# Two weight-tail loads laid out with an outermost extent of 8 in a one-core decode kernel

## The chip, the cores and the metric

The kernel runs on one core of a Trainium2 chip. A time is the device time of one execution in microseconds. Before and after were each run 6 times beside each other; the experiments were timed 4 times each, beside 7 runs of the kernel before on the same chip. A ratio is the mean time of one kernel's fast runs over that of the other's of the same rounds, so it is not quite the ratio of the medians quoted. A span in the profile leaves out some 2 us at the ends (before: 382.6 us span, 384.72 us median).

Besides the views of the profile I use the trace's records of single DMA packets (start, duration, bytes, queue). A packet here is one row: 32768 B for keys and values, 36864 B for the main rows of gate, up and wo, 4608 B for the last 64 rows of gate and up ("the tails"), 10368, 6912 and 3456 B for W_down. A 4 B packet is the completion write of one DMA engine for one load. The records do not name the engine. I chained them by their times (a row starts within a few ns of the end of the one before on the same engine) and by the order of the queue; chains can swap engines that stand within some ns of each other. Packet sums by engine below, and which engines carried what, rest on that; packet durations do not.

## The reference, cut to what matters

```python
def reference(A_x, A_k_cache, A_v_cache, A_wq, A_wo, B_x, B_W_gate, B_W_up, B_W_down):
    x = A_x                                        # 4 rows of 576
    h = x + attention(layernorm(x), ...)           # 32 heads, 16 KV heads, window of 4096 of 16384
    # second block, all weights bf16
    n = layernorm(h)
    gate = n @ B_W_gate                            # 576 x 4608
    up = n @ B_W_up                                # 576 x 4608
    return h + (where(gate > 0, gate, 0) * up) @ B_W_down    # 4608 x 576
```

128 MiB of keys and values and about 25 MB of weights are read once, for 4 rows of input.

## The kernel before: the parts that matter

All large loads go to one queue in program order: keys and values in 32 loads of 4 MiB (wq after the first), with wo before the last value load, then gate, up and W_down. A weight of 576 rows is split: its first 512 rows lie four to a partition, its last 64 are cut in halves and fill all 128 partitions.

```python
def main_rows(W):
    return W[0:512, :].rearrange("(p r) n -> p (r n)", r=4)

def last_rows(W):
    return W[512:576, :].rearrange("r (a n) -> (r a) n", a=2)     # partition 2r + a
...
# add_kv: outermost extent of the source 32, four partitions to each
src = cache[b, 4 * qd:4 * qd + 4, SK - WIN:SK, :].rearrange("a (p t) d -> p a (t d)", p=32)
...
for g, W in ((0, B_W_gate), (1, B_W_up)):
    for m, n, src in ((1, F // 2, last_rows(W)), (0, 4 * F, main_rows(W))):
        gu_off[(g, m)] = off
        place(("gu", g, m), off, n, ("GU", g, m),
              lambda e, off=off, n=n, src=src: e.dma_start(out=arena[:, off:off + n], in_=src))
        off += n
...
# the tail's input chunk is masked, once for each half a of the row
for a in range(2):
    dve("n3", lambda e, a=a: e.tensor_scalar(out=hnT[:, 4 + a, 0:4], in0=tmp5[:, 4, :],
                                             scalar1=par[:, a:a + 1], scalar2=None, op0=ALU.mult), ...)
```

Of the kernel before, what the change touches and what calls it, by code (L numbers as in the profile page):

```python
# [6 lines left out]
ALU = mybir.AluOpType  # L7
AX = mybir.AxisListType
FP32 = mybir.dt.float32
BF16 = mybir.dt.bfloat16  # L10

B = 4
D = 576
# [5 lines left out]
F = 4608  # L19
# [95 lines left out]
def bass_sequential_preLN__sliding_block_cached__glu_gated_reglu__decode_kernel(  # L115
# [12 lines left out]
    with ExitStack() as es:  # L128
        cnt = [0]

        def sb(name, shape, dt):
            return es.enter_context(nc.sbuf_tensor("sb_" + name, shape, dt))
# [3 lines left out]
        dve = lambda name, fn, deps=(): P.op("vector", name, fn, deps)  # L136
# [12 lines left out]
        c_qm = sb("c_qm", [128, 4, 32], FP32)  # L149
# [2 lines left out]
        perm = sb("perm", [128, 4, 32], BF16)  # L152
        m4 = sb("m4", [128, 4], FP32)
        par = sb("par", [128, 2], FP32)
        am8 = sb("am8", [128, 8], FP32)
        qm = sb("qm", [128, 4], FP32)
        e8 = sb("e8", [128, 8], FP32)
# [5 lines left out]
        warm = sb("warm", [128, 2], FP32)  # L163
        x_bf = sb("x_bf", [B, D], BF16)
        xn_bf = sb("xn_bf", [B, D], BF16)
        xd_bf = sb("xd_bf", [B, 64, 2], BF16)
        xnd_bf = sb("xnd_bf", [B, 64, 2], BF16)
        bn = sb("bn", [B, 2, 6], FP32)
        mv = sb("mv", [B, 8], FP32)
# [11 lines left out]
        hnT = sb("hnT", [128, DC + 1, 32], BF16)  # L181
        R_sb = sb("R_sb", [128, DC, 2, B], FP32)
        st2 = sb("st2", [128, 40], FP32)
        tmp5 = sb("tmp5", [128, DC, B], FP32)
# [6 lines left out]
        partd = pp[:, 1152:1408].bitcast(FP32)  # L191
# [7 lines left out]
        psb = es.enter_context(nc.psum_tensor("psb", [128, 8, 512], FP32))  # L199
# [39 lines left out]
                  lambda e: e.dma_start(out=arena[:, off:off + TILE], in_=src), key=f"slot{s}")  # L239


        def main_rows(W):
            return W[0:512, :].rearrange("(p r) n -> p (r n)", r=4)

        def last_rows(W):
            return W[512:576, :].rearrange("r (a n) -> (r a) n", a=2)

        P.dma("scalar", ("L", "x"), lambda e: e.dma_start(out=x_bf[:, :], in_=A_x.rearrange("b s d -> (b s) d")), "d_x")
        add_kv("K", 0)
# [17 lines left out]
        gu_off = {}  # L267
        off = WO_OFF + H * D
        for g, W in ((0, B_W_gate), (1, B_W_up)):
            for m, n, src in ((1, F // 2, last_rows(W)), (0, 4 * F, main_rows(W))):  # L270
                gu_off[(g, m)] = off
                place(("gu", g, m), off, n, ("GU", g, m), lambda e, off=off, n=n, src=src: e.dma_start(out=arena[:, off:off + n], in_=src))
                off += n
        WDJ = 9 * D
        wd_off = []
        for j in range(4):
            wd_off.append(off)
            for r0, r1 in ((0, 9),) if j < 3 else ((0, 6), (6, 9)):
                place(("wd", j, r0), off + r0 * D, (r1 - r0) * D, "DOWN",
                      lambda e, off=off, j=j, r0=r0, r1=r1: e.dma_start(  # L280
                          out=arena[:, off + r0 * D:off + r1 * D],
                          in_=B_W_down[j * 1152:(j + 1) * 1152, :].rearrange("(p r) n -> p (r n)", p=128)[:, r0 * D:r1 * D]))
            off += WDJ

        def kv(kind, i):
# [24 lines left out]
                                                in_=c_qm[:, :, :].rearrange("p q (h j) -> p q h j", j=4),  # L310
# [20 lines left out]
        for q in range(4):  # L331
# [9 lines left out]
                                               op0=ALU.mult, op1=ALU.add), ["c_par0"])  # L341
        dve("c_am8", lambda e: e.tensor_copy(out=am8[:, :].rearrange("p (a h) -> p a h", h=2),
                                             in_=bass.AP(tensor=m4, offset=0, ap=[[4, 128], [1, 4], [0, 2]])), ["c_m4"])
# [4 lines left out]
        for hf in range(2):  # L348
# [6 lines left out]
                                            op0=ALU.subtract, op1=ALU.mult), ["rstd"])  # L355
        act("warm_exp", lambda e: e.activation(out=warm[:, 1:2], in_=eps_c[:, :], func=ACT.Exp), ["std"])

        dve("xd", lambda e: e.tensor_copy(out=xd_bf[:, :, :], in_=bass.AP(tensor=x_bf, offset=512, ap=[[D, B], [1, 64], [0, 2]])))
        dve("xnd", lambda e: e.tensor_copy(out=xnd_bf[:, :, :], in_=bass.AP(tensor=xn_bf, offset=512, ap=[[D, B], [1, 64], [0, 2]])),
            ["xn"])  # L360

# [1 line left out]
        def chunk(t, td, c):  # L363
            return td if c == 4 else t[:, 0:512].rearrange("b (p r) -> b r p", r=4)[:, c, :]
# [3 lines left out]
        def pe_q():  # L368
            for c in range(DC):
                pe("TP0", lambda e, c=c: e.transpose(out=tpv[:, c * 4:(c + 1) * 4],  # L370
                                                     in_=chunk(xn_bf, xnd_bf[:, :, :].rearrange("b r a -> b (r a)"), c),
                                                     identity=ident_b[0:B, 0:B]), ["xnd", "xd", "c_idb"] if c == 0 else [])
            for c in range(DC):
                pe("TP1", lambda e, c=c: e.transpose(out=tpv[:, 32 + c * 4:32 + (c + 1) * 4],
                                                     in_=chunk(x_bf, xd_bf[:, :, :].rearrange("b r a -> b (r a)"), c),
                                                     identity=ident_b[0:B, 0:B]))
            for c in range(DC):
                for n in range(8):
                    g, bk = n % 4, n // 4
                    w = arena[:, wq_off + c * H * DH + n * 512:][:, 0:512] if c < 4 else pT[:, n % 4 * 512:n % 4 * 512 + 512]  # L380
                    pe("QMM", lambda e, c=c, w=w, g=g, bk=bk: e.matmul(
                        bank[4 + bk][32 * g:32 * g + 32, :], lhsT=xnT[:, c + bk if c == 4 else c, :], rhs=w,
                        start=(c == 0), stop=(c == DC - 1), skip_group_check=True),
                        ([("L", "wq", c // 4)] + (["xnT", "c_xnT"] if c == 0 else [])) if n == 0 and c % 4 == 0 else [])
            for bk in range(2):
                for s in range(4):
                    blk = bk * 4 + s
                    pe(("QT", blk), lambda e, blk=blk: e.transpose(out=mb_ps[:, blk * 128:(blk + 1) * 128],
                                                                   in_=p_sb[:, blk * 128:(blk + 1) * 128], identity=ident_b[:, :]),
                       [f"qev{bk}"] if s == 0 else [])  # L390
# [17 lines left out]
        def act_q():  # L408
            act("qev1", lambda e: e.copy(out=p_sb[:, 512:1024], in_=bank[5]), ["QMM"])
# [152 lines left out]
        for s in range(NUNIT + 16):  # L562
            b, k = divmod(s - 16, 16)
            if b >= 0 and k == 3:
                put_pT(b, 2)
            if s < NUNIT:
                pe_tr(s)
                for j in range(4):
                    evac(s, j)
            if b >= 0 and k == 1:  # L570
                softmax(b, 1)
            if s == 3:
                pe_q()
                act_q()
                dve_q()
                dve("c_qm", lambda e: e.tensor_reduce(out=qm[:, :], in_=c_qm[:, :, :], axis=AX.X, op=ALU.max), ["c_qm1"])
                dve("c_e8", lambda e: e.tensor_reduce(out=e8[:, :], in_=c_e8[:, :, :], axis=AX.X, op=ALU.max), ["c_e81"])
                dve("c_sel", lambda e: e.tensor_reduce(out=sel4[:, 0:4], in_=c_s4[:, :, :], axis=AX.X, op=ALU.max),
                    ["c_s41", "c_sel0"])
                for q in range(4):  # L580
                    dve("c_selc", lambda e, q=q: e.tensor_copy(out=selc[:, q, :, q], in_=e8[:, :]), ["c_e8", "c_selc0"])
                pe_qk(0)
            elif s >= 4 and s % 2 == 0 and s // 2 - 1 < NUNIT // 2:
                dd = s // 2 - 1
                pe_qk(dd)
                if dd % 8 == 7:
                    softmax(dd // 8, 0)
            if b >= 0:
                if k == 0 and b:
                    finish_o(b - 1)  # L590
                elif 1 <= k <= 3:
                    put_pT(b, (0, 1, 3)[k - 1])
                elif 4 <= k < 8:
                    weights(b, k - 4)
                if k % 4 == 3:
                    for w in range(4):
                        pe_pv(s - 19 + w)
                    select_o((s - 19) // 4)
# [5 lines left out]
        for a in range(8):  # L604
            for j in range(4):
                for n in range(2):
# [3 lines left out]
                        [("ONORM", B - 1), ("L", "wo"), ("EV", NUNIT - 1, 0), ("EV", NUNIT - 1, 1)] if a == j == n == 0 else [])  # L610
        dve("part0", lambda e: e.tensor_copy(out=part[:, 0:288], in_=bank[0][:, 0:288]), ["WO", ("PV", NUNIT - 1)])
        act("part1", lambda e: e.copy(out=part[:, 288:576], in_=bank[1][:, 0:288]), ["WO", ("PV", NUNIT - 1)])  # L612
        dve("partd", lambda e: e.tensor_copy(out=partd.rearrange("p (r a) -> p r a", a=2),
                                             in_=bass.AP(tensor=psb, offset=512 + 224, ap=[[4096, 128], [1, 64], [0, 2]])), ["part1"])
        for c in range(DC):
            pe("HT", lambda e, c=c: e.matmul(m_ps[:, c * 4:(c + 1) * 4], lhsT=chunk(part, partd, c), rhs=sel4[:, 0:4],
                                             start=True, stop=True), ["part0", "part1", "partd", "c_sel"] if c == 0 else [])
# [1 line left out]
                                            in1=xT[:, :, :], op=ALU.add), ["HT", "xT"])  # L619
# [16 lines left out]
        dve("n2a", lambda e: e.tensor_tensor(out=tmp5[:, :, :], in0=tmp5[:, :, :], in1=rstd_bc, op=ALU.mult), ["n1", "s6"])  # L636
        dve("n2", lambda e: e.tensor_copy(out=hnT[:, 0:4, 0:4], in_=tmp5[:, 0:4, :]), ["n2a", "c_hnT"])
        for a in range(2):
            dve("n3", lambda e, a=a: e.tensor_scalar(out=hnT[:, 4 + a, 0:4], in0=tmp5[:, 4, :], scalar1=par[:, a:a + 1], scalar2=None,  # L639
                                                     op0=ALU.mult), ["n2a", "c_hnT"])  # L640


        for g in range(2):
# [16 lines left out]
        for m in range(3):  # L660
            dve(("HH", m), lambda e, m=m: e.tensor_tensor(out=hh[:, m * 384:(m + 1) * 384], in0=bank[3 + m][:, 0:384],  # L661
                                                          in1=g_sb[:, m * 384:(m + 1) * 384], op=ALU.mult),
# [29 lines left out]
        for n in range(4):  # L692
            P.dma("sync" if n % 2 == 0 else "scalar", ("O", n),
                  lambda e, n=n: e.dma_start(out=orow[:, 144 * n:144 * (n + 1)], in_=out_sb[32 * n:32 * n + 4, :]), f"d_out{n}", ["OUT"])
# [30 lines left out]
```

## Time and profile before

| | before |
|---|---|
| median (6 runs) | 384.72 us (384.55 to 384.99) |
| HBM read | 159.58 MB |
| DMA, 35 to 347 us | busy share 1.00, 429 GB/s |
| last DMA wait of the chain | 32.18 us |
| 4608 B packet of a tail | 0.178 to 0.188 us |
| spread of the 16 completions of the last load | 6.6 us |

The page of the kernel before. The two rows of 40 are equal slices of the span (9.6 us each): mean busy share of the 16 DMA engines in tenths, and what they moved.

```profile
span 382.6 us, 8170 instructions
...
DMA  8999999999999999999999999999999999999992
GB/s 329 439 433 432 410 421 437 434 433 433 425 423 433 427 433 435 427 420 433 437 430 435 424 428 427 427 428 439 437 432 415 421 436 451 416 431 426 416 411 113
DMA packets 6408, 160.09 MB, mean 418 GB/s; under 512 B 740, under 2 KB 744, under 8 KB 1384
...
q1 hardware_dynamic: 6352, 159.59, 97.4%
q8 instruction: 29, 0.48, 0.5%
```

The engines are busy from the first slice to the last but one, at a nearly constant rate. Nothing but the loads bounds this kernel. The chain of waits from 312 us on, kernel before (start, duration, what):

```profile
312.11 30.05 DMA sb_arena<-in_A_v_cache_dram
...
347.17 32.18 DMA sb_arena<-in_B_W_down_dram
...
379.40 0.58 PE psb L687 x12
...
380.00 0.31 DVE sb_out_sb L690
```

Once the last load has landed, 0.58 us of matmuls, a copy of 0.31 us and the store remain. So the kernel ends when the *slowest* DMA engine has done its rows. Stretches, kernel before (last two columns: DMA busy share and GB/s):

```profile
335.00:348.00 13.00, 3.95 (x56) 1.47 (x60) 1.71 (x2) 0.00 (x0) 0.00 (x0) 0.50 0.99 424
348.00:353.00 5.00, 4.36 (x88) 2.71 (x79) 0.46 (x2) 0.16 (x1) 0.00 (x0) 0.50 1.03 436
353.00:368.00 15.00, 9.80 (x112) 6.86 (x116) 2.48 (x14) 1.70 (x5) 0.00 (x0) 0.62 0.99 421
368.00:380.00 12.00, 6.14 (x195) 4.00 (x185) 2.24 (x5) 0.27 (x1) 0.00 (x0) 0.92 0.62 260
```

The busy share of 0.62 in the last row is an imbalance: by the packet records eight engines have written the last completion 4.9 to 6.6 us after the first one, the other eight up to 2.1 us after it. By the chains the late ones are those that also carry the 29 instruction packets of queue 8 (16384 B, about 1.07 us each). Such a packet holds the engine's data back by 1 us, and the row after it takes 1.68 to 1.76 us instead of 1.215: about 1.55 us lost each time, three or four times for each of these eight engines.

### The profile page before, as it was taken

How to read it: one execution, taken by the hardware profiler on the slowest of the kernel's cores; microseconds unless marked ns; L12 is line 12 of the kernel's file. 1: busy time of each engine (PE TensorE's matmuls, PEld its weight loads, DVE VectorE, ACT ScalarE, POOL GpSimd, SP SyncE). 2: the span in 40 equal slices, each digit the busy share in tenths (PEclk: the TensorE clock that was granted, in tenths of full speed). 3: DMA queues.
4: the chain of work that ended last, by engine and by line, in shares of the span. 5: the costliest groups of instructions: out<-in, count | busy, mean ns of one | idle time of the engine just before them, and what ended most of it. 6: DMA issues, size and time to landing. Idle time of an engine off the chain costs nothing.

```text
span 382.6 us, 8170 instructions
## 1 busy us (share of the span) xinstructions
PE 248.7 (65%) x3781; PEld 185.9 (49%) x3781; DVE 159.0 (42%) x277; ACT 146.4 (38%) x162; POOL 8.7 (2%) x36
## 2 busy tenths in 40 slices
PE   0664999779492938893947667966759366026753
PEld 0643788557371726672726455745546222003532
DVE  3342565665342434774432426752516454002220
ACT  3341688836161524762433428542525401000010
POOL 7100000000000000000000000000000000000000
PEclk9997999999888796999796969996969657555597
DMA  8999999999999999999999999999999999999992
GB/s 329 439 433 432 410 421 437 434 433 433 425 423 433 427 433 435 427 420 433 437 430 435 424 428 427 427 428 439 437 432 415 421 436 451 416 431 426 416 411 113
DMA packets 6408, 160.09 MB, mean 418 GB/s; under 512 B 740, under 2 KB 744, under 8 KB 1384
## 3 DMA queue, kind: packets, MB, share of 16 engines
q1 hardware_dynamic: 6352, 159.59, 97.4%
q8 instruction: 29, 0.48, 0.5%
q14 instruction: 3, 0.02, 0.0%
q10 hardware_dynamic: 24, 0.01, 0.0%
HBM read 159.58 MB, written 0.00 MB: 417 GB/s over the span
## 4 chain that ended last, share of the span: by engine, by line
DMA 69%; PE 27%; DVE 2%; SPq 1%; ACT 1%; issue 0%
DMA sb_arena<-in_A_k_cache_dram 53%; PE psb L425 18%; DMA sb_arena<-in_B_W_down_dram 8%; DMA sb_arena<-in_A_v_cache_dram 8%; PE psb L457 5%; PE psb L505 2%; PE psb L480 1%; DVE sb_pp L487 1%; ACT sb_pp L468 1%; SPq L280 0%; DVE sb_stat L464 0%; DVE sb_o_sel L516 0%; PE psb L539 0%; PE psb L530 0%; DVE sb_o_tmp L512 0%
## 5 line engine op out<-in xcount | busy, mean ns | idle before, releaser
L425 PE MATMUL psb<-sb_perm,sb_arena 128*128 128x128 bf16 x2048 | 140.3, 235 | 74.0 <-DMA sb_arena<-in_A_k_cache_dram 73.8
L441 ACT COPY sb_arena<-psb 128x1024 bf16<-128x1024 bf16 x128 | 123.0, 1021 | 141.1 <-PE psb L425 141.1
L425 PEld LDWEIGHTS psb<-sb_perm,sb_arena 128*128 128x128 bf16 x2048 | 131.5, 106 | 89.3 <-DMA sb_arena<-in_A_k_cache_dram 79.8
L439 DVE COPY sb_arena<-psb 128x1024 bf16<-128x1024 bf16 x128 | 87.0, 689 | 112.1 <-PE psb L425 111.6
L505 PE MATMUL psb<-sb_arena,sb_pp 128*32 128x512 bf16 x512 | 35.9, 425 | 19.9 <-DMA sb_arena<-in_A_v_cache_dram 19.9
L457 PE MATMUL psb<-sb_arena,sb_qTm 128*32 128x512 bf16 x512 | 38.0, 423 | 0.9 <-DVE sb_qTm L404 0.9
L505 PEld LDWEIGHTS psb<-sb_arena,sb_pp 128*32 128x32 bf16 x512 | 12.9, 104 | 36.3 <-DMA sb_arena<-in_A_v_cache_dram 20.9
L512 DVE TENSOR_TENSOR sb_o_tmp<-psb,sb_qm 128x512 f32<-128x512 f32 x16 | 11.1, 692 | 41.2 <-PE psb L505 41.2
L487 DVE TENSOR_TENSOR sb_pp<-psb,sb_am 128x1024 bf16<-128x1024 bf16 x16 | 19.6, 1223 | 16.2 <-PE psb L480 16.2
L480 PE MATMUL psb<-sb_ident_b,sb_pp 128*128 128x128 bf16 x128 | 11.5, 242 | 15.8 <-DVE sb_pp L487 8.3
L468 ACT ACTIVATE sb_pp<-psb,sb_stat 128x2048 bf16<-128x2048 f32 x8 | 15.8, 1975 | 9.7 <-DVE sb_stat L466 9.7
L457 PEld LDWEIGHTS psb<-sb_arena,sb_qTm 128*32 128x32 bf16 x512 | 11.6, 103 | 14.8 <-issue 6.2
L480 PEld LDWEIGHTS psb<-sb_ident_b,sb_pp 128*128 128x128 bf16 x128 | 8.6, 108 | 18.8 <-ACT sb_pp L468 8.1
L516 DVE TENSOR_REDUCE sb_o_sel<-sb_o_tmp 128x128 f32<-128x512 f32 x16 | 16.4, 1024 | 0.5
L612 ACT COPY sb_pp<-psb 128x288 f32<-128x288 f32 x1 | 0.4, 399 | 36.2 <-PE psb L607 36.2
L654 PE MATMUL psb<-sb_arena,sb_hnT 128*32 128x384 bf16 x120 | 7.5, 421 | 4.1 <-DVE sb_hnT L639 2.2
L654 PEld LDWEIGHTS psb<-sb_arena,sb_hnT 128*32 128x32 bf16 x120 | 4.1, 121 | 7.2 <-DMA sb_arena<-in_B_W_up_dram 2.3
L464 DVE TENSOR_REDUCE sb_stat<-psb 128x1 f32<-128x1024 f32 x4 | 4.9, 1221 | 4.6 <-PE psb L457 4.6
L687 PE MATMUL psb<-sb_arena,sb_pp 128*32 128x144 bf16 x144 | 3.7, 251 | 4.1 <-DMA sb_arena<-in_B_W_down_dram 3.6
L534 ACT ACTIVATE sb_stat<-sb_stat 128x1 f32<-128x1 f32 x4 | 0.9, 213 | 13.1 <-DVE sb_stat L532 13.1
L661 DVE TENSOR_TENSOR sb_pp<-psb,sb_pp 128x384 bf16<-128x384 f32 x3 | 1.5, 551 | 9.6 <-PE psb L654 9.6
L687 PEld LDWEIGHTS psb<-sb_arena,sb_pp 128*32 128x32 bf16 x144 | 2.6, 105 | 5.1 <-DMA sb_arena<-in_B_W_down_dram 4.6
(128 smaller groups left out, 78.7 us busy)
## 6 DMA issues: line engine op xcount, KB each, us to landing
sb_arena<-in_A_k_cache_dram SPq DMA_DIRECT2D x16, 4096.0 KB, 28.3
sb_arena<-in_A_v_cache_dram SPq DMA_DIRECT2D x16, 4096.0 KB, 33.6
sb_arena<-in_A_wo_dram SPq DMA_DIRECT2D x1, 4608.0 KB, 20.7
sb_arena<-in_B_W_gate_dram SPq DMA_DIRECT2D x1, 4608.0 KB, 34.1
sb_arena<-in_B_W_up_dram SPq DMA_DIRECT2D x1, 4608.0 KB, 43.5
sb_arena<-in_A_wq_dram SPq DMA_DIRECT2D x1, 4096.0 KB, 23.0
sb_arena<-in_B_W_down_dram SPq DMA_DIRECT2D x3, 1296.0 KB, 30.0
sb_arena<-in_B_W_down_dram SPq DMA_DIRECT2D x1, 864.0 KB, 31.6
```

The lines of the kernel that those rows point to most:

```text
L425: o = pe(("TRJ", i, j), lambda e, j=j, u=u, t=t: e.transpose(out=bankb[TRB[j]][:, u * 128:(u + 1) * 128], in_=kn[:, t, :], identity=perm[: ...
L439: dve(("EV", i, j), lambda e: e.tensor_copy(out=dst, in_=src), deps)
L441: act(("EV", i, j), lambda e: e.copy(out=dst, in_=src), deps)
L457: o = pe(("QK", dd), lambda e, a=a, j=j: e.matmul(bank[4 + w][32 * j:32 * j + 32, :], lhsT=qTm[:, b, 4 * qd + a, :], rhs=k[:, j, :, a, :], ...
L468: act(("EXP", b, w), lambda e: e.activation(out=p_sb[:, 2048 * w:2048 * w + 2048].rearrange("p (k a) -> p k a", a=4), in_=bass.AP(tensor=p ...
L480: pe(("PT", b, r), lambda e, tl=tl: e.transpose(out=mb_ps[:, tl * 128:(tl + 1) * 128], in_=p_sb[:, (r * 8 + tl) * 128:(r * 8 + tl + 1) * 128],
L487: dve(("PM", b, r), lambda e: e.tensor_tensor(out=dst, in0=src, in1=msk, op=ALU.mult), [("PT", b, r), "c_am8", ("PV", 16 * b - 1) if b els ...
L505: pe(("PV", i), lambda e, j=j, lo=lo, pm=pm, tb=tb: e.matmul(o_ps[32 * j:32 * j + 32, :], lhsT=pT[:, pm:pm + 32], rhs=v[:, lo:lo + 512], s ...
L512: dve(("OS", g), lambda e: e.tensor_tensor(out=o_tmp[:, :].rearrange("p (t d) -> p t d", t=4), in0=o_ps.rearrange("p (t d) -> p t d", t=4) ...
L516: dve(("OSEL", g), lambda e: e.tensor_reduce(out=o_sel[:, qd, :], in_=o_tmp[:, :].rearrange("p (t d) -> p d t", t=4), axis=AX.X, op=ALU.ad ...
L654: pe(("GU", g, c // 4), lambda e, g=g, m=m, j=j, lo=lo, c=c: e.matmul(bank[3 * g + m][32 * j:32 * j + 32, 0:384], lhsT=hnT[:, c if c < 4 e ...
L687: pe("DOWN", lambda e, j=j, r=r, n=n, wv=wv: e.matmul(bank[0][32 * n:32 * n + 32, 0:144], lhsT=hhT[:, r * 128 + 32 * j:r * 128 + 32 * j + 32],
```

## The change

The intent is to let only half of the DMA engines carry the two tails. For that the source pattern gets an outermost extent of 8, which needs another order of the rows over the partitions (partition 32x + 16a + y holds half a of row 4y + x), and so another mask and reordered copies of the input chunk. The diff, cut to its core:

```diff
+        par8 = sb("par8", [128, 2], FP32)
...
-        xd_bf = sb("xd_bf", [B, 64, 2], BF16)
+        xd_bf = sb("xd_bf", [B, 4, 2, 16], BF16)
...
+        def last_rows8(W):
+            return W[512:576, :].rearrange("(y x) (a n) -> (x a) y n", x=4, a=2)
...
-            for m, n, src in ((1, F // 2, last_rows(W)), (0, 4 * F, main_rows(W))):
+            for m, n, src in ((1, F // 2, last_rows8(W)), (0, 4 * F, main_rows(W))):
...
+                dve("c_par80", lambda e: e.tensor_tensor(out=par8[:, 1:2], in0=qm[:, 2:3], in1=qm[:, 3:4], op=ALU.add), ["c_qm"])
+                dve("c_par8", lambda e: e.tensor_scalar(out=par8[:, 0:1], in0=par8[:, 1:2], scalar1=-1.0, scalar2=1.0,
+                                                        op0=ALU.mult, op1=ALU.add), ["c_par80"])
...
-        dve("partd", lambda e: e.tensor_copy(out=partd.rearrange("p (r a) -> p r a", a=2),
-                                             in_=bass.AP(tensor=psb, offset=512 + 224, ap=[[4096, 128], [1, 64], [0, 2]])), ["part1"])
+        dve("partd", lambda e: e.tensor_copy(out=partd.rearrange("p (x a y) -> p x a y", x=4, a=2),
+                                             in_=bass.AP(tensor=psb, offset=512 + 224, ap=[[4096, 128], [1, 4], [0, 2], [4, 16]])), ["part1"])
...
-            ... scalar1=par[:, a:a + 1], ... ["n2a", "c_hnT"])
+            ... scalar1=par8[:, a:a + 1], ... ["n2a", "c_hnT", "c_par8"])
```

More of the change, by code (lines that the diff above doesn't have):

```diff
@@ L356, in bass_sequential_preLN__sliding_block_cached__glu_gated_reglu__decode_kernel @@
         act("warm_exp", lambda e: e.activation(out=warm[:, 1:2], in_=eps_c[:, :], func=ACT.Exp), ["std"])
-        dve("xd", lambda e: e.tensor_copy(out=xd_bf[:, :, :], in_=bass.AP(tensor=x_bf, offset=512, ap=[[D, B], [1, 64], [0, 2]])))
+        dve("xd", lambda e: e.tensor_copy(out=xd_bf[:, :, :, :],
+                                          in_=bass.AP(tensor=x_bf, offset=512, ap=[[D, B], [1, 4], [0, 2], [4, 16]])))
         dve("xnd", lambda e: e.tensor_copy(out=xnd_bf[:, :, :], in_=bass.AP(tensor=xn_bf, offset=512, ap=[[D, B], [1, 64], [0, 2]])),
@@ L374, in pe_q @@
                 pe("TP1", lambda e, c=c: e.transpose(out=tpv[:, 32 + c * 4:32 + (c + 1) * 4],
-                                                     in_=chunk(x_bf, xd_bf[:, :, :].rearrange("b r a -> b (r a)"), c),
+                                                     in_=chunk(x_bf, xd_bf[:, :, :, :].rearrange("b x a y -> b (x a y)"), c),
                                                      identity=ident_b[0:B, 0:B]))
@@ L638, in bass_sequential_preLN__sliding_block_cached__glu_gated_reglu__decode_kernel @@
         for a in range(2):
-            dve("n3", lambda e, a=a: e.tensor_scalar(out=hnT[:, 4 + a, 0:4], in0=tmp5[:, 4, :], scalar1=par[:, a:a + 1], scalar2=None,
-                                                     op0=ALU.mult), ["n2a", "c_hnT"])
+            dve("n3", lambda e, a=a: e.tensor_scalar(out=hnT[:, 4 + a, 0:4], in0=tmp5[:, 4, :], scalar1=par8[:, a:a + 1], scalar2=None,
+                                                     op0=ALU.mult), ["n2a", "c_hnT", "c_par8"])
         for g in range(2):
```

## The prediction

> **What bounds it now.** The DMA engines. The page counts 159.59 MB on the sync queue at 97.4% of the 16 engines' span. By stretches, DMA is 1.00 busy from 35 to 347 us (429 GB/s) and 0.88 from 347 to 379 us. In the chain of waits, one DMA wait of 32.18 us (347.17 to 379.35, on the last W_down rows) ends the kernel; behind it stand only 0.58 us of matmuls, a 0.31 us copy and the store. The 0.88 means that at the end some engines are idle.
>
> **Imbalance.** In the trace's records of single DMA packets, the 16 completion writes of the last W_down load spread over 6.6 us, in two groups of eight: 0.0, 0.2, 0.3, 0.3, 0.4, 0.8, 2.1 (one more near 0.3) and 4.9, 5.0, 5.1, 6.4, 6.5, 6.5, 6.6, 6.6 us. Queue 8 (instructions) carries 29 packets of 16 KB, each about 1.07 us. Each stops one engine's data for about 1 us, and the row after it takes about 1.70 us instead of 1.215: about 1.55 us lost. They go round eight engines only, so five engines carry four and three carry three (6.2 and 4.7 us): the late group.[...]
>
> **What the change does.** The same 1.18 MB of gate and up tails, 256 rows of 4608 B, 0.180 us each. Now every engine has 8 rows of each, about 1.43 us with the completion write. [...] So eight engines gain 2 x 1.43 = 2.86 us and eight lose as much. Added on VectorE: two tiny mask operations near 22 to 40 us and reshaped copies (0.20 and 0.29 us before), all hidden under DMA waits. Neither traffic nor TensorE work changes.
>
> **On the critical path.** Everything rests on whether the eight instruction-laden engines are the upper half. If so: the late group ends at 6.6 - 2.86 = 3.74; the early group at 0.8 + 2.86 = 3.66, its worst (2.1, itself hit by three 8 KB instruction packets) at 4.95. The end moves by about 1.65 us: 383.1 us. If the laden ones are the lower half, or are mixed across halves, a laden engine gains 2.86 us: 387.6. The trace doesn't name engines. For the upper half: the early group were mostly also the first to complete the first key load, and the shift (5.7 us between the groups) fits the imbalance. I give it about 0.78.
>
> **Predicted:** 383.2 us; range 382.0 to 387.8, skewed to the fast end. Faster by over 2%: 0.005; within: 0.985; slower: 0.01.
>
> **What would show it.** Rows of 4608 B: eight engines with 16 each per tensor, none on the others. Completion spread of the last load about 2 us instead of 6.6; DMA share between 347 us and the end near 0.95; the last DMA wait about 30.5 us. Wrong half: spread near 9.5 us with the same two groups. The chain before 347 us and every VectorE wait should be unchanged.
>
> **What would make it wrong.** The half; write contention[...]; strided instead of contiguous reads slowing the 4608 B packets (0.180 us); a different distribution of instruction packets in unprofiled runs.

That an extent of 8 means eight engines was an assumption at this point; the result shows it. Counted from the first completion in the kernel before, the last engine was to end at 4.95 us instead of 6.6, 1.65 us earlier: 383.1 instead of 384.72 us (383.2 us predicted). A clause that says where write contention would arise, which was not shown either, is cut from the last paragraph. "Upper half" means the eight engines that carry no tail after the change, "lower half" the eight that do.

## The result

| | before | after |
|---|---|---|
| median (6 runs each) | 384.72 us | 397.50 us (396.59 to 398.85) |
| ratio | 1 | 1.0333 (95%: 1.0311 to 1.0356) |
| 4608 B packets, median (longest) | 0.180 us (0.188) | 0.307 us (0.412) |
| 36864 B packets of gate and up, mean (longest) | 1.372 us (1.869) | 1.775 us (2.458) |
| spread of the last completions | 6.6 us | 11.3 us |

The change made the kernel 3.3% slower, far outside the range. The page of the kernel after:

```profile
span 394.4 us, 8172 instructions
...
DMA  7999999999999999999999999999999999999991
GB/s 319 425 434 460 418 434 424 425 424 427 434 430 435 430 424 437 427 427 435 430 427 424 429 434 427 429 442 430 429 424 424 430 441 420 267 374 254 375 393 63
DMA packets 6392, 160.09 MB, mean 406 GB/s; under 512 B 724, under 2 KB 728, under 8 KB 1368
...
q1 hardware_dynamic: 6336, 159.59, 97.0%
q8 instruction: 29, 0.48, 0.5%
```

Three things stand here. There are 16 packets fewer: eight engines write no completion for either tail, so eight engines carry the tails, as meant. The bytes are the same. And two dips have appeared in the GB/s row (267 and 254 in slices 35 and 37 of 9.9 us), while the busy row above still reads 9: the engines are busy, but with slower packets. The stretches of the kernel after show it more sharply:

```profile
335.00:348.00 13.00, 1.55 (x16) 0.63 (x20) 0.00 (x0) 0.00 (x0) 0.00 (x0) 0.50 1.04 281
348.00:353.00 5.00, 2.73 (x55) 1.03 (x48) 2.01 (x3) 0.00 (x0) 0.00 (x0) 0.50 0.94 406
353.00:368.00 15.00, 11.47 (x138) 8.11 (x138) 2.64 (x14) 0.60 (x2) 0.00 (x0) 0.61 1.02 287
368.00:380.00 12.00, 2.27 (x31) 0.77 (x30) 0.00 (x0) 1.25 (x3) 0.00 (x0) 0.64 0.95 401
```

DMA share 1.04 at 281 GB/s, against 0.99 at 424 before. The chain of waits of the kernel after:

```profile
312.08 34.33 DMA sb_arena<-in_A_v_cache_dram
...
351.42 39.96 DMA sb_arena<-in_B_W_down_dram
...
391.43 0.40 PE psb L696 x12
...
391.85 0.31 DVE sb_out_sb L699
```

The wait for the last W_down rows grew by 7.8 us, and the wait for the last value load, issued before the tails, by 4.3 us. The second is no contradiction: the early engines are in the gate tail while the late ones still have value rows to load.

Chained by engine, the one that ends last can be laid beside the last one of before. From the completion of wo to its last completion (us):

| leg of the last engine | before | after | difference |
|---|---|---|---|
| completion of wo on this engine, from the span's start | 330.52 | 330.50 | -0.02 |
| last value load | 9.72 | 12.58 | +2.86 |
| gate tail | 1.42 | 4.79 | +3.37 |
| gate main rows (before: with one instruction packet, 1.55) | 12.48 | 14.56 | +2.08 |
| up tail | 1.43 | 4.77 | +3.34 |
| up main rows | 10.92 | 11.28 | +0.36 |
| W_down | 12.45 | 12.45 | 0.00 |
| sum | | | +11.99 |

The spans differ by 11.8 us (the last matmuls took 0.18 us less after), so this is where the time came from. The tails take 6.71 us more. Of that 2.86 us are the doubled rows that the prediction priced; 3.85 us are rows that became slow. The other loads of the same engine lost 5.3 us, or about 6.85 us without the instruction packet that only the kernel before has there.

In the kernel after, all engines lose while *any* engine is in a tail. From 343.63 to 347.38 us, by the chains, only two engines were still in the gate tail (their rows took about 0.29 us). The 13 packets of 36864 B that the others started up to 345.50 us took 2.18 to 2.35 us, against 1.37 us before. So it isn't only that the eight engines get in each other's way.

### The profile page after: what moved, and what is told of

Same layout as the page of the kernel before. It is cut to its first block, busy times and chain, and to the rows that moved or that the text cites. A ratio compares the mean times of both kernels' runs of the same rounds, so it can differ in the third digit from the quotient of the medians.

```text
span 394.4 us, 8172 instructions
## 1 busy us (share of the span) xinstructions
PE 250.8 (64%) x3781; PEld 186.1 (47%) x3781; DVE 159.5 (40%) x279; ACT 146.4 (37%) x162; POOL 8.7 (2%) x36
## 2 busy tenths in 40 slices
DMA packets 6392, 160.09 MB, mean 406 GB/s; under 512 B 724, under 2 KB 728, under 8 KB 1368
## 4 chain that ended last, share of the span: by engine, by line
DMA 70%; PE 26%; DVE 2%; SPq 1%; ACT 1%; issue 0%
DMA sb_arena<-in_A_k_cache_dram 51%; PE psb L431 17%; DMA sb_arena<-in_B_W_down_dram 10%; DMA sb_arena<-in_A_v_cache_dram 9%; PE psb L463 5%; PE psb L511 2%; PE psb L486 1%; DVE sb_pp L493 1%; ACT sb_pp L474 1%; SPq L285 0%; DVE sb_stat L470 0%; DVE sb_o_sel L522 0%; PE psb L545 0%; PE psb L536 0%; PE psb L529 0%
## 5 line engine op out<-in xcount | busy, mean ns | idle before, releaser
L511 PE MATMUL psb<-sb_arena,sb_pp 128*32 128x512 bf16 x512 | 37.3, 438 | 22.7 <-DMA sb_arena<-in_A_v_cache_dram 22.7
L511 PEld LDWEIGHTS psb<-sb_arena,sb_pp 128*32 128x32 bf16 x512 | 13.2, 107 | 40.7 <-DMA sb_arena<-in_A_v_cache_dram 24.6
L486 PE MATMUL psb<-sb_ident_b,sb_pp 128*128 128x128 bf16 x128 | 11.3, 239 | 15.8 <-DVE sb_pp L493 8.3
L663 PE MATMUL psb<-sb_arena,sb_hnT 128*32 128x384 bf16 x120 | 9.9, 516 | 11.9 <-DMA sb_arena<-in_B_W_up_dram 9.7
```

What stands on the lines that cost most here:

```text
L486: pe(("PT", b, r), lambda e, tl=tl: e.transpose(out=mb_ps[:, tl * 128:(tl + 1) * 128], in_=p_sb[:, (r * 8 + tl) * 128:(r * 8 + tl + 1) * 128],
L511: pe(("PV", i), lambda e, j=j, lo=lo, pm=pm, tb=tb: e.matmul(o_ps[32 * j:32 * j + 32, :], lhsT=pT[:, pm:pm + 32], rhs=v[:, lo:lo + 512], s ...
L663: pe(("GU", g, c // 4), lambda e, g=g, m=m, j=j, lo=lo, c=c: e.matmul(bank[3 * g + m][32 * j:32 * j + 32, 0:384], lhsT=hnT[:, c if c < 4 e ...
```

## The experiments

The theories at the start are these. **P, placement:** what counts is how the partitions are dealt out to the engines. With extent 128 one outermost index is one partition, with extent 8 it is 16 neighbouring ones. **S, stride:** the new pattern reads rows 36864 B apart. **C, compute:** the added VectorE work. **K:** eight engines carrying a load are slow in themselves.

Two names come in later: **P1**, two engines that write one group of partitions share its bandwidth and nobody else is hurt; **P2**, any write outside an engine's own group slows every engine. The partitions of e4 to e6, e8, e9 and e11 to e13 were chosen on the assumption that each engine has partitions of its own. That was not shown: no record names the engine or the partitions of a packet. The runs themselves show only which loads, by extent and partitions, were fast and which were slow. All experiments but c1 start from the kernel before. "Wrong on purpose" means that other rows, or too few, are loaded. Where only the tails' 64 rows were exchanged the comparison with the reference still passed, since they weigh little; e5, e6 and e11 load half of them and failed it.

### e1: extent 8, contiguous reads, no new compute

```diff
+        def tail_src(W):
+            return W[504:576, :].rearrange("(e r) (a n) -> e (r a) n", e=8, a=2)[:, 0:16, :]
...
-            for m, n, src in ((1, F // 2, last_rows(W)), ...
+            for m, n, src in ((1, F // 2, tail_src(W)), ...
```

> The kernel before, with only the gate and up tail loads replaced: outermost extent 8, but each engine reads its sixteen 4608 B rows from one contiguous stretch (rows 504 to 575 of the weight in groups of nine, eight of them read; the result is wrong on purpose). Theory P (placement: an engine's sixteen rows go to sixteen consecutive partitions[...]): as after, 396 to 399 us, 4608 B packets near 0.31 us, the other engines' 36864 B packets above 2 us. Theory S (the strided reads of the new layout are what is slow): packets 0.18 us and about 387.6 us, from two instruction-laden engines that carry 2.86 us more. Theory C (the added mask and copies on VectorE): about 387.6 us too.

Measured: 397.44 us, ratio 1.0327 (1.0312 to 1.0342). 4608 B packets 0.308 us, 36864 B packets 1.773 us in the mean. Two of the page's lines for e1:

```profile
GB/s 320 425 424 454 441 427 424 421 427 424 437 427 435 434 424 437 427 424 432 430 434 424 426 430 430 425 439 434 435 424 424 426 445 417 270 374 254 374 391 67
DMA packets 6392, 160.09 MB, mean 406 GB/s; under 512 B 724, under 2 KB 728, under 8 KB 1368
```

The same two dips, the same time. The stride and the VectorE work are out: the extent of 8 alone is the whole effect.

### e2: extent 128, strided reads

```diff
+            return W[64:576, 0:F // 2].rearrange("(p r) n -> p r n", r=4)[:, 0, :]
```

> The kernel before, with the tail loads read at a stride of 36864 B between neighbouring partitions (rows 64, 68, ... first half; wrong result on purpose), outermost extent still 128. P: no change, 384.7 us, 4608 B packets 0.18 us. S: slow, packets near 0.3 us and the other packets near 2 us, 390 us or more.

Measured: 384.82 us, ratio 1.0001 (0.9986 to 1.0016); packets 0.179 us. A stride of 36864 B costs nothing here. S is refuted from the other side too.

### e3: extent 16

```diff
+            return W[496:576, :].rearrange("(e r) (a n) -> e (r a) n", e=16, a=2)[:, 0:8, :]
```

> The kernel before, with the tail loads given an outermost extent of 16 (rows 496 to 575 in groups of five, the first four of them read, contiguous for an engine; wrong result on purpose). All 16 engines carry 8 rows each[...]. P: slow although all engines take part, 4608 B packets above 0.22 us, 388 to 395 us. S, and the rival K (eight engines instead of sixteen is what hurts): 384.7 us, packets 0.18 us.

Measured: 392.97 us, ratio 1.0211 (1.0193 to 1.0229). Two lines of its page:

```profile
GB/s 323 430 428 430 425 426 438 425 431 431 436 428 428 431 428 436 431 423 430 425 428 433 439 428 428 425 425 430 435 438 431 433 419 445 351 321 307 370 409 121
DMA packets 6408, 160.09 MB, mean 410 GB/s; under 512 B 740, under 2 KB 744, under 8 KB 1384
```

The packet count is that of before, so all 16 engines carry 8 rows of each tail, and yet 4608 B packets take 0.316 us (up to 0.541) and 36864 B packets up to 2.882 us. So K isn't needed for the slowness; that eight engines are not slow in themselves is shown by e5 and e11 below.

### e4: extent 8, in loads of eight partitions

Each tail as 16 loads of eight partitions, four apart.

```diff
+                    for p0 in [b + i for b in (0, 32, 64, 96) for i in range(4)]:
+                        P.dma("sync", ("L", "gu", g, m),
+                              lambda e, ...: e.dma_start(out=arena[p0:p0 + 29:4, off:off + n], in_=src[p0:p0 + 29:4, :]), ...)
```

> The kernel before, with each tail load cut into 16 loads of eight partitions four apart (right result), outermost extent 8, so the same eight engines should carry all of it[...]. P: packets of the loads to the lower partitions 0.18 us, those to the upper ones[...] up to 0.35 us; in all 387 to 391 us. K or S: all packets near 0.3 us and 396 us or more.

Measured: 394.23 us, ratio 1.0244 (1.0227 to 1.0261), above what was expected. The packets fit P: the first eight loads (partitions below 64) run at 0.178 us a row, with nobody slowed, and as soon as the loads to partitions 64 and up begin, the same engines' rows take about 0.35 us, twice as long. But the 14 value packets (32768 B) that started from 0.4 us before that moment to 2 us after it all took 1.87 to 2.36 us, on eight engines by the chains, two of them of the lower half (the eight engines that carry tails). So the other six were slowed without carrying a tail, and that is why the time was underestimated.

### e5 and e6: the same loads, four partitions apart

e5 keeps only the half of e4 that ran fast (first partitions 0 to 3 and 32 to 35); e6 shifts it by four.

```diff
-                    for p0 in [b + i for b in (0, 32) for i in range(4)]:
+                    for p0 in [b + i for b in (4, 36) for i in range(4)]:
```

> Only the 64 rows of each tail that go to partitions 0 to 31 and 32 to 63 are loaded (8 loads of eight partitions four apart a tail; half the bytes, wrong result on purpose), outermost extent 8[...]. The eight engines carry 8 rows a tail, as before, the other eight none. Placement theory: 4608 B packets all 0.18 us, 36864 B packets 1.37 us, and 384.7 us, since the last engine is one of the two instruction-laden ones of the eight and carries what it carried before. If eight engines instead of sixteen were slow in themselves: packets 0.3 us, near 390 us.

> The same loads, moved up by four partitions (4 to 35 and 36 to 67)[...]. Theory P1 (two engines that write one group of partitions share its bandwidth, nothing else): 4608 B packets 0.18 us while all eight are in the tail, 0.36 us beside a neighbour's other packets, the upper engines' packets unchanged; 385 to 389 us. Theory P2 (a write outside the engine's own group slows every engine): all packets slow, 36864 B ones of all engines near 2 us, 389 us or more.

Measured: e5 383.95 us, ratio 0.9981 (0.9962 to 1.0000), all 4608 B packets 0.178 to 0.185 us (two of its four runs stand near 383.3 and two near 384.6 us, which is not explained). e6 390.47 us, ratio 1.0157 (1.0138 to 1.0175), packets 0.320 us, 36864 B packets up to 2.514 us. Lines of the page of e5, then of e6:

```profile
GB/s 331 440 401 430 433 433 439 426 428 421 433 432 432 435 421 433 428 432 432 418 435 437 432 431 421 421 433 437 435 430 416 430 428 456 424 415 430 421 409 123
DMA packets 6376, 159.50 MB, mean 419 GB/s; under 512 B 836, under 2 KB 840, under 8 KB 1352
```

```profile
GB/s 325 432 431 432 428 429 431 428 431 431 432 426 429 427 427 432 427 426 429 427 431 432 428 431 431 431 431 432 431 431 431 432 426 436 357 400 308 405 392 68
DMA packets 6376, 159.50 MB, mean 411 GB/s; under 512 B 836, under 2 KB 840, under 8 KB 1352
```

Same bytes, same number of engines and of loads; only the partitions, and with them the rows read, moved by four. The rows read aren't the reason: e5 and e11 (below) read all of e6's rows, and e11 those of e4's slow loads, at 0.178 us (e11's 4544 B packets 0.175). This pair shows the placement to be the cause. In e6 the eight value packets that started between 1.7 and 3.7 us after the first tail packet averaged 2.10 us, against 1.22 us without the tail: nearly everybody is slow, as P2 expected.

### e7: one engine alone

One load more, of 61 rows of 2560 B, meant for one engine.

```diff
+                if (g, m) == (0, 1):
+                    place(("xx",), 80640, 1280, ("GU", 0, 0), lambda e, ...: e.dma_start(out=arena[0:61, xo:xo + 1280], in_=W[0:61, 0:1280]))
```

> The kernel before and one load more, after the up tail: 61 rows of 2560 B to partitions 0 to 60 of spare columns. [...] It needs 61 x 0.10 = 6 us on its own. P1: at any time it shares with at most one engine, so of the others' packets only one in fifteen is slow, and its own packets are up to 0.2 us. P2: the packets of all 15 others are near 2 us (36864 B) for as long as it runs. Time: 390 to 397 us if that engine is one of the two laden ones or slows down the others, near 384.7 to 391 us if it is one of the early ones.

(The recorded text says "after the up tail"; the edit puts the load after the gate tail. Its 0.10 us a row is an estimate from 0.180 us for 4608 B. That one engine would carry all rows was an assumption.) Measured: 397.31 us, ratio 1.0324, but this time means little: the spare columns were not free yet, the load waited for them and held up the queue behind it, and the DMA engines stood idle (0.33 busy from 340 to 348 us). The packets still say something. One completion packet more than in the kernel before (713 against 712 on the queue) shows that one engine carried the load. While the 61 rows ran (8.4 us, median 0.133 us a row), the 52 packets of 36864 B that the others started from 1.2 to 7 us after their beginning took 1.52 to 2.08 us, median 1.63, instead of 1.37; after them 1.37 again. The packets of the first 1.2 us are left out, because they follow idle time: also at the start of the kernel before the first 16 packets take 1.47 to 2.13 us instead of 1.215. One engine slowed all the others by a fifth. That is neither P1 (one in fifteen) nor P2 as I had put it (near 2 us).

### c1: the gate tail alone

```diff
-            ... last_rows8(W) ...
+            ... last_rows8(W) if g == 0 else last_rows(W) ...
```

> The kernel after, with only the gate tail at extent 8 and the up tail loaded as before (wrong result, since the up tail's rows are then in the other order; all of the new VectorE work is in). Placement theory: one slow stretch instead of two, about half of the 12.8 us, 390 to 392 us. If the added VectorE work cost time by itself: above that.

Measured: 390.44 us, ratio 1.0143 (1.0124 to 1.0161). 5.8 of the 12.8 us: one dip instead of two.

### e8 and e9: two engines, in the steady stretch

Eight loads more of two partitions each into a new tensor, after the ninth key load (an extent of 2 is taken as two engines, as 8 was eight in the kernel after; likewise 4 in e13); e9 starts four partitions higher.

```diff
+            if g == 8:
+                for p0 in [b + i for b in (0, 32) for i in range(4)]:      # e9: (4, 36)
+                    P.dma("sync", ("L", "xx"), lambda e, p0=p0: e.dma_start(out=xx[p0:p0 + 5:4, :], in_=xsrc[p0:p0 + 5:4, 0:4096]), "d_xx")
```

> The kernel before and, in the steady stretch after the ninth key load, 8 small loads more of two partitions each, four apart (partitions 0 to 7 and 32 to 39 of a new tensor, rows of 8192 B, right result): outermost extent 2, so two engines carry 8 rows each[...]. Both P1 and P2: no other engine's packet changes (32768 B stays 1.215 us), 8192 B packets 0.31 us. Time: 384.7 us, or up to 387.2 us if one of the two engines is instruction-laden.

> The same 8 loads moved up by four partitions (4 to 11 and 36 to 43)[...]. P1 (sharing only): at most the packets of two other engines get longer, the 13 others stay at 1.215 us. P2 (every engine is slowed while any engine writes outside its group): the 32768 B packets of nearly all 16 engines get longer, to 1.4 us and more, for as long as the 8192 B packets run, and these take more than 0.31 us. Time under P2 1 to 4 us above e8.

Measured: e8 384.89 us (ratio 1.0003), e9 384.89 us (1.0002), both the same as before. The packets differ:

| | 8192 B packets, median | 32768 B packets started from 1.3 us before the first of them to the last one's end | up to 1.23 us | 1.23 to 1.40 | 1.40 to 1.90 | over 1.90 |
|---|---|---|---|---|---|---|
| e8, partitions 0 to 7 and 32 to 39 | 0.309 us | 53 | 53 | 0 | 0 | 0 |
| e9, 4 to 11 and 36 to 43 | 0.545 us | 80 | 46 | 32 | 0 | 2 |
| e12, moving | 0.443 us | 54 | 6 | 13 | 35 | 0 |
| e13, four engines, 4 to 19 and 36 to 51 | 0.402 us | 81 | 8 | 53 | 18 | 2 |

In e9 two packets doubled (2.27 and 2.42 us), and the rest got up to 9% longer (1.32 us) while both engines were in it, nothing but the second of the two doubled ones once only one was left (the others 1.21 to 1.23 us). P2 fails for the two engines of e9.

### e10: extent 32

```diff
+            return W[416:576, :].rearrange("(e r) (a n) -> e (r a) n", e=32, a=2)[:, 0:4, :]
```

> The kernel before with the tail loads given an outermost extent of 32 (groups of five rows of which two are read, four partitions a group; wrong result on purpose), as the key and value loads have it. If what counts is that a share is one aligned group of four partitions: as before, 384.7 us, 4608 B packets 0.18 us. If any extent below 128 misplaces rows: slow, as with 16 (393 us).

Measured: 384.86 us, ratio 1.0002 (0.9987 to 1.0017); packets 0.179 us. With extent 32 one outermost index is one aligned group of four partitions, as in the key and value loads; the packets are as fast as with extent 128 (0.180 us).

### e11: all of the tails on eight engines, at e5's partitions

e5 and eight loads more a tail, into a spare tensor at partitions below 64.

```diff
+                    for p0 in [b + i for b in (0, 32) for i in range(4)]:
+                        P.dma("sync", ("L", "xx", g), lambda e, ...: e.dma_start(out=xx[p0:p0 + 29:4, 2272 * g:2272 * g + 2272],
+                                                                                  in_=src[64 + p0:64 + p0 + 29:4, 0:2272]), "d_xx")
```

> e5 and, for the other 64 rows of each tail, 8 loads more into a spare tensor at the same partitions below 64 (rows of 4544 B; wrong result on purpose): the same eight engines carry all the tails' bytes, as the change meant[...]. Placement theory: packets 0.18 us, nobody slowed, and what is left is the shift of 2.86 us onto eight engines, two of them instruction-laden: 386.5 to 388 us. If carrying everything on eight engines is itself slow: 395 us or more.

Measured: 386.90 us, ratio 1.0055 (1.0031 to 1.0078); 4608 B packets 0.178 to 0.185 us. Its stretches and its last wait:

```profile
335.00:348.00 13.00, 3.81 (x47) 1.32 (x51) 1.71 (x2) 0.00 (x0) 0.00 (x0) 0.50 1.02 434
353.00:368.00 15.00, 9.37 (x86) 6.32 (x86) 1.92 (x12) 1.46 (x4) 0.00 (x0) 0.66 0.97 413
```

```profile
347.31 33.13 DMA sb_arena<-in_B_W_down_dram
```

434 and 413 GB/s, no dips. This is what the change meant to do. It costs 2.1 us, by the chains because two of the eight engines are among those that carry the instruction packets. (The four runs stand at two levels, 386.0 and 387.7 us, which is not explained; the profiled one is of the lower, so its last wait is only 0.95 us above that of before.) So even with fast rows the idea loses here; of the 12.8 us it explains about a sixth.

### e12 and e13: moving partitions, or more engines

It was open why engines are slowed that carry none of the slow rows.

```diff
-                for p0 in [b + i for b in (4, 36) for i in range(4)]:       # e9
+                for p0 in (4, 12, 20, 37, 45, 53, 6, 14):                   # e12
...
-                    ... out=xx[p0:p0 + 5:4, :], in_=xsrc[p0:p0 + 5:4, 0:4096] ...      # e9
+                    ... out=xx[p0:p0 + 13:4, :], in_=xsrc[p0:p0 + 13:4, 0:4096] ...    # e13
```

> e9 with the 8 loads' first partitions changed to 4, 12, 20, 37, 45, 53, 6, 14: the same two engines and bytes[...]. If a misplaced writer hurts only the owner of the group it is writing[...]: each row delays one owner, about 16 packets of 32768 B longer than 1.4 us in all, the others 1.22 to 1.32 us. If it is the moving from group to group that slows every engine: most of the 32768 B packets that start while the 8192 B packets run are above 1.4 us. Time 384.7 to 387 us in either case; the packets decide.

> e9 with four engines instead of two (loads of four partitions four apart, from 4 to 7 and 36 to 39)[...]. If the loss of the others grows with the number of misplaced engines (e9: up to 8% with two while both ran; the eight of e6: 70%): the 32768 B packets of the engines that are not written to reach 1.4 to 1.9 us while the four run. If it needs moving targets: they stay at or below 1.32 us and only the owners' packets exceed 2 us. Time 384.7 to 388 us.

Measured: e12 385.76 us (ratio 1.0026, 1.0009 to 1.0043), e13 386.07 us (1.0033, 1.0018 to 1.0048). The rows of the table above show that more is slowed in both than in e9. In e12 two engines write other partitions with each load, and 35 of 54 packets exceed 1.4 us (up to 1.83), none over 1.9. Sixteen rows were written, so it is not one slowed packet for each row. In e13 four engines, whose partitions do not jump like this, slow 18 packets to 1.4 us and more (up to 1.79 apart from the doubled ones, while all four run). But the number of engines isn't all: once only one of the four was left, the packets that the others started from 3.9 to 5.9 us after the first row still took 1.29 to 1.42 us, where one left in e9 slowed one packet only. The tail loads of the changed kernel may do both: eight engines carry the 256 rows of both tails, in the mean 16 a tail each, and if each takes one outermost index (not shown), these go to 16 neighbouring partitions.

## Why the prediction was wrong

1. **The bound: right.** The loads bound the kernel and the slowest engine ends it; the last DMA wait was still the chain's end after (39.96 us), with 0.40 us of matmuls behind it.
2. **The extent of 8 puts the tails on eight engines: right.** 16 completion packets fewer (6392 packets against 6408).
3. **"eight engines gain 2 x 1.43 = 2.86 us": this is the step that failed.** It took the duration of a row (0.180 us) from an extent of 128 and kept it for one of 8. The rows took 0.307 us; the last engine's two tails took 9.56 us instead of 5.71 (2.85 before plus 2.86).
4. **"Neither traffic nor TensorE work changes": true, and not enough.** The sum had no term for the other packets. Gate and up main rows went from 1.372 to 1.775 us in the mean, and the last value load of the last engine from 9.72 to 12.58 us. I named write contention among what could make the prediction wrong, but gave it no price, no probability, and no place in the range. Of the 12.8 us lost, the 10.7 us that e11 did not lose come from this step and the one before.
5. **"For the upper half ... about 0.78": wrong.** In the changed kernel six of the eight early engines carry tails and two do not, so of the eight instruction-laden ones two are in the lower half and six are not. My branch for that case said 387.6 us; e11, with rows of 0.178 to 0.185 us, measured 386.9. With fast rows this part of the sum held within 0.7 us.
6. **VectorE work hidden: right.** e1 without it takes 397.44 us, the changed kernel 397.50.
7. **"The chain before 347 us ... should be unchanged": wrong,** by 4.3 us, since engines run several us apart and the early ones slow the late ones.

What is settled: the cause is how the partitions are dealt out to the engines. Before, e1, e3 and e10 fill the same 128 partitions, at extents of 128, 8, 16 and 32, with rows of 0.180, 0.308, 0.316 and 0.179 us; e5 and e6 differ in the partitions (0.178 to 0.185 against 0.320 us) and in the rows read, which were fast in e5 and e11. What stays open is how this slows engines that carry none of the slow rows. The share of packets over 1.4 us was larger with more engines and with partitions that change from load to load (e9 2 of 80, e13 20 of 81, e12 35 of 54), but neither alone accounts for it: a single engine slowed one packet only at the end of e9 and all the packets beside it by 6 to 17% at the end of e13 (1.29 to 1.42 us against 1.215). The runs show no path on which this could happen. Which engine wrote which partition is not shown either. I have no version that beats the kernel before. Perfect balance could gain some 3.3 us (an estimate from the 16 completion times of the last load: the last is 6.6 us after the first, their mean 3.3 us), and the eight engines that an extent of 8 picks include two of the late ones. Extent 2 at e8's partitions carried 131 KB more at no cost (384.89 us), but moving the tails there was not tried.

## What to carry to other kernels

When you change the outermost extent of a load, you change not only how many engines carry it: here a 4608 B row took 0.18 us at extents of 32 and 128 and 0.31 to 0.32 us at 8 and 16, over the same 128 partitions, and 0.18 us again at 8 on other partitions (e5, e11). So check the duration of the load's packets, and that of the packets beside them. Read GB/s beside the busy share: a DMA row that stays at 9 while the rate falls from 424 to 281 GB/s is no sign of full speed: the packets have become slow, and every load in flight pays. And when a sum uses a duration from the trace, ask whether the change leaves alone what that duration depended on; if you list a cause that could break it, price it.
